# A fused attention and mixture-of-depths kernel: rows of four batches transposed by TensorE in place of DMA, their one-hot rows made by GpSimd, and a new hand-written order

## The chip, the cores and the metric

The kernel runs on one core of one Trainium2 chip. A core has five engines with an instruction stream each: TensorE (PE in the profile, with its weight loads as PEld), VectorE (DVE), ScalarE (ACT), GpSimd (POOL) and SyncE (SP). They work side by side and wait for each other by semaphores. Sixteen DMA engines move data for all of them; a DMA is issued by one of the instruction streams (here POOL for nearly all loads and stores, SP for the transposes). The metric is the device time of one execution in microseconds, lower is better.

## The reference

Eight batches of twelve heads, a sequence of 448 and a head size of 64. The attention takes the square of a Relu in place of a softmax:

```
scores = q k^T / 8
attn   = max(scores, 0)^2 / 448
x      = attn v            # heads side by side: [8, 448, 768]
```

On x, a mixture of depths follows. For each batch, 128 of the 448 tokens (those with the highest gate score `x . w_gate`) go through an MLP, and its result is added to their rows:

```
s   = x . w_gate                       # [8, 448]
idx = the 128 largest of s[b]
ye  = max(x[b, idx] w1, 0) w2          # 768 -> 1024 -> 768
out = x;  out[b, idx] += sigmoid(s[b, idx]) * ye
```

Inputs and output are fp32; the kernel works in bf16 with fp32 accumulation.

## The kernel before, in words

**Units.** The attention is cut into 24 units of four heads (u = 0 to 23), three to a batch. The sequence is cut into NC = 7 chunks of 64 keys. Each unit goes through these steps, named as in the order list:

- `Lq`, `Lk`, `Lv` (L95 to L105): GpSimd issues the loads, with a cast from fp32 to bf16. q, k and v tiles come from rings of seven buffers, so the load for unit u + 7 must wait until unit u's tile has been read by PE.
- `T` (L194): 28 groups of small PE transposes turn q and k into PSUM; `TE` copies them to SBUF (`qkt`, L131 or L135, in the helper `put`).
- `S` (L213): the score matmuls of one chunk, `R` (L131): Relu from PSUM to SBUF by ScalarE, 168 in all; `Q` (L228): the square by VectorE, for chunks 0 to 3 and 4 to 6 of a unit; `V` (L237): the matmul with v; `X` (L131 or L137): the result out of PSUM, scaled, as columns of x transposed (`xT_sb`, [feature, token]).
- `XB` (L258): two DMA transposes issued by SP bring the unit's 256 features from `xT_sb` into row form (`x_sb`, [token, feature]). Functions `XT` and `XE`, which would do this by TensorE and an eviction, exist in the code and are not in the order.

**Batches.** When the three units of a batch are through, the class `Moe` handles it: `g` (L297) gate scores by matmul, replicated over partitions; `bc` and `col`/`colE` (L306) bring them to SBUF as rows and as columns; `rk` (L316) gives each token's rank by comparing its score with all others; `hot` (L322) makes a one-hot row for each token by comparing its rank with 1 to 128; `sel` (L329) turns that into row numbers; `xe` (L341) gathers the chosen rows by a matmul of `x_sb` with the one-hot matrix, and `xeE` evicts them; `h` (L360), `hE`, `gt` (L372), `sig`, `y` (L382) and `yE` are the MLP with its gate. `ST` (L278) stores the rows of x, two DMAs a batch, and `ADD` (L392) adds the MLP's rows to the output in DRAM by an indirect, accumulating DMA.

`xe` needs the whole batch in `x_sb`, and so all six transposes of the batch, as well as the four `hot` rows.

**The order.** The schedule is manual. One list, `ORDER`, names every step of every engine in the order in which it is issued: each engine, and each queue, executes its own steps in the order of the list, and a step that waits holds up everything behind it on the same engine. The arguments say what is worked on and where: `S,4,3,6` is the scores of unit 4, chunk 3, into PSUM banks 6 and 7; `R,4,3` its Relu; a last letter A, D or P names ScalarE, VectorE or GpSimd. PSUM has eight banks, and the list says which step uses which. All data of one batch flows through a chain across engines (PE, ACT, DVE, DMA, PE), so the list interleaves several units and batches.

Of the kernel before, what the change touches and what calls it, by code (L numbers as in the profile page):

```python
# [19 lines left out]
def kernel(  # L20
# [178 lines left out]
    def TE(u, part=None, eng="D"):  # L199
        if u not in qkt:  # L200
            qkt[u] = qt_pool.tile([128, 2, 2, NC, P], BF16, name="qkt")
        for s in range(2) if part is not None else (slice(0, 2),):
            w = (slice(None), s) if part is None else (slice(None), s, part)
            r = "p s t c n -> p s (t c n)" if part is None else "p c n -> p (c n)"
            put(eng, qkt[u][w].rearrange(r), t_ps[u][w].rearrange(r))
# [11 lines left out]
    GROUPS = ((0, 1, 2, 3), (4, 5, 6))  # L217

    def R(u, c, eng="A"):
        g = [i for i, cs in enumerate(GROUPS) if c in cs][0]  # L220
        if (u, g) not in r_sb:
            r_sb[u, g] = r_pool.tile([128, len(GROUPS[g]), 2, S], BF16, name=f"r_sb{len(GROUPS[g])}")
        put(eng, r_sb[u, g][:, GROUPS[g].index(c)], s_ps.pop((u, c))[:, :, :S], func=AF.Relu)

    def Q(u, g):
        r = r_sb.pop((u, g))
        a = a_sb[u, g] = a_pool.tile([128, len(GROUPS[g]), 2, S], BF16, name=f"a_sb{len(GROUPS[g])}")
        nc.vector.tensor_tensor(out=a, in0=r, in1=r, op=ALU.mult)  # L228

    def V(u, g, at=None):  # L230
        if g == 0:
            o_ps[u] = banks(at, 2)
        for i, c in enumerate(GROUPS[g]):
            a = a_sb[u, g][:, i]
            for s, j, bank, col in ((0, 0, 0, 0), (1, 0, 0, 1), (1, 1, 1, 0), (0, 1, 1, 1)):
# [1 line left out]
                nc.tensor.matmul(out=o_ps[u][64 * col:64 * col + 64, bank, :S],  # L237
                                 lhsT=v_sb[u][rows, j, c, :], rhs=a[rows, j, :], start=(c == 0),
                                 stop=(c == NC - 1), skip_group_check=True)
# [169 lines left out]
    colE,0,D V,3,0,4 rk,0,3 R,4,3 S,4,4,1 V,3,1 rk,0,1 R,4,4 T,5,0,6 hot,0,3,D Lv,10,0 hot,0,1,D X,3,A rk,0,0
    S,4,2,2 S,4,5,0 R,4,2 rk,0,2 S,4,6,4 T,5,1 R,4,5 hot,0,0,D hot,0,2,D Lk,12 TE,5 xe,0,3,1,3 R,4,6  # L410
    xe,0,0,1,2 Lv,6,1 xe,0,4,1 xe,0,1,1 xe,0,5,1 Lv,7,0 xe,0,2,1 xeE,0,D,1 sel,0,7 xeE,0,A,0 S,5,3,5 Lq,9
    Q,4,1 S,5,0,0 gt,0,4 R,5,0 Lv,7,1 h,0,0,1,3 h,0,4,1,2 sig,0 Lq,10 h,0,1,1 R,5,3 Q,4,0 h,0,5,1 S,5,2,0
    S,5,1,5 h,0,6,1 R,5,1 h,0,2,1 selE,0,D h,0,7,1 R,5,2 h,0,3,1 V,4,0,4 hE,0,A,0 Q,5,0 hE,0,A,1 S,5,4,0
    S,5,5,6 V,4,1 R,5,4 T,6,0,2 X,4,A S,5,6,0 T,6,1 R,5,6 XB,4 g,1,0,1,5 TE,6 y,0,0,0,2,4 R,5,5 g,1,1,1
    y,0,0,2,2 Q,5,1 S,6,0,0 S,6,1,2 V,5,0,6 R,6,0 R,6,1 y,0,0,4,2 S,6,2,0 V,5,1 R,6,2 T,7,0,2 X,5,D Lv,12,0
    S,6,3,0 T,7,1 Lv,9,0 R,6,3 XB,5 g,1,2,1 TE,7 Lq,11 y,0,0,6,2 bc,1,A S,6,5,6 yE,0,A,0 Lk,10 XB,3 Q,6,0
    col,1 R,6,5 S,6,4,2 y,0,1,0,2,4 R,6,4 S,6,6,0 y,0,1,2,2 R,6,6 S,7,1,6 colE,1,D S,7,0,2 rk,1,0 y,0,1,4,2
    R,7,1 T,8,0,0 rk,1,3 R,7,0 S,7,2,6 rk,1,2 y,0,1,6,2 R,7,2 T,8,1 rk,1,1 S,7,4,2 yE,0,A,1 S,7,5,6 R,7,4 TE,8
    S,7,6,4 R,7,5 S,7,3,2 hot,1,2,D S,8,1,0 Q,6,1 R,7,3 V,6,0,6 R,7,6 S,8,3,2 Q,7,0 V,6,1 R,8,1 T,9,0,4
    Lv,13,1 X,6,A T,9,1 Lv,10,1 R,8,3 hot,1,0,D S,8,0,6 hot,1,3,D V,7,0,0 hot,1,1,D Lk,14 TE,9 R,8,0  # L420
    xe,1,3,1,3 Lv,8,0 xe,1,0,1,2 Q,7,1 S,8,6,4 Lk,16 S,8,2,6 R,8,6 xe,1,1,1 xe,1,4,1 Lq,13 xe,1,2,1 R,8,2
    xe,1,5,1 xeE,1,D,0 S,9,0,4 Lk,11 V,7,1 xeE,1,A,1 S,8,4,6 Lq,14 R,9,0 X,7,D h,1,4,1,2 h,1,0,1,3 Lv,12,1
    R,8,4 h,1,5,1 Q,8,0 XB,7 S,8,5,4 S,9,2,0 S,9,1,6 R,8,5 h,1,1,1 h,1,6,1 XB,6 R,9,2 h,1,2,1 h,1,7,1 Q,8,1
    R,9,1 T,10,0,4 h,1,3,1 hE,1,A,1 sel,1,0 hE,1,D,0 gt,1,7 T,10,1 selE,1,D sig,1 S,9,3,2 TE,10 Lk,17 S,9,6,0
    R,9,3 y,1,0,0,2,6 g,2,0,1,7 Lv,9,1 R,9,6 y,1,0,2,2 Q,9,0 Lv,11,1 S,10,0,4 V,8,0,2 R,10,0 S,9,4,0 V,8,1
    R,9,4 S,9,5,4 X,8,D Lv,15,1 y,1,0,4,2 R,9,5 S,10,1,0 ST,0,1 g,2,1,1 R,10,1 Q,9,1 XB,8 y,1,0,6,2 Lq,12
    S,10,3,2 S,10,2,4 R,10,3 T,11,0,0 Lv,15,0 yE,1,D,0 T,11,1 R,10,2 ST,1,0 S,10,4,2 TE,11 y,1,1,0,2,6 R,10,4
    Lv,11,0 g,2,2,1 y,1,1,2,2 Q,10,0 bc,2,A ST,0,0 S,10,6,4 S,11,1,0 R,10,6 y,1,1,4,2 Lk,18 col,2 y,1,1,6,2
    R,11,1 Lv,14,0 S,11,0,4 V,9,0,2 colE,2,D yE,1,A,1 Lk,13 rk,2,2 R,11,0 S,10,5,6 V,9,1 rk,2,1 R,10,5 Lv,16,0
    rk,2,0 T,12,0,0 X,9,A S,11,2,4 rk,2,3 T,12,1 R,11,2 S,11,3,2 hot,2,0,D V,10,0,6 hot,2,1,D R,11,3 hot,2,2,D  # L430
    hot,2,3,D TE,12 xe,2,0,1,5 xe,2,3,1,4 S,11,4,2 xe,2,1,1 Q,10,1 R,11,4 xe,2,4,1 xe,2,2,1 xe,2,5,1 xeE,2,A,0
    S,11,5,0 S,11,6,2 xeE,2,D,1 V,10,1 R,11,6 h,2,0,1,5 X,10,A Lv,17,1 sel,2,4 XB,9 h,2,4,1,3 R,11,5 selE,2,D
    Lv,13,0 h,2,1,1 Q,11,0 S,12,1,6 Lq,15 h,2,2,1 R,12,1 h,2,5,1 Lq,17 h,2,3,1 h,2,6,1 Q,11,1 hE,2,A,0 ST,2,0
# [99 lines left out]
```

## Time and profile before

| | |
|---|---|
| median of three runs | 256.56 us (255.26 to 257.10) |
| the profiled execution | 256.13 us |
| its span, first to last instruction | 254.4 us |
| mean granted TensorE clock | 0.881 of full speed |
| mean DMA rate | 162 GB/s, 41.11 MB |

How to read it: the span is cut by engine. Busy time is the time in which an engine executes instructions; what an engine waited for is listed beside the instruction that waited, with the tile that came last. A row such as `x_sb<-xT_sb` names the tile written and the tile read. The chain of waits is followed back from the last instruction; a piece on it isn't necessarily time in which nothing else happened, so it is compared with the timeline of the engine that waited. In tables by stretch, the last three columns are the granted TensorE clock (1.00 is full speed), the DMA load (packet time over the time of 16 engines; over 1 when packets of several queues overlap) and GB/s.

### The profile page before, as it was taken

The numbers are of one execution on the slowest core, as the hardware profiler recorded it, in microseconds if no ns is written. First come the engines' busy times: TensorE is split into PE (matmuls) and PEld (weight loads), VectorE is DVE, ScalarE is ACT, GpSimd is POOL, SyncE is SP. The second block draws the span as 40 slices with busy tenths as digits, with TensorE's granted clock in tenths as the row PEclk, the third lists the DMA queues.
The fourth block names the chain that finished last, engine by engine and source line by source line (L and its number), as shares of the span: only waits on it lengthen the run. The fifth ranks groups of instructions, "written<-read, shape, count | busy, mean of one in ns | idle before, by whom it ended". The sixth has DMA issues, their size and how long they took to land.

```text
span 254.4 us, 8167 instructions
## 1 busy us (share of the span) xinstructions
PE 190.4 (75%) x3614; PEld 118.4 (47%) x3614; DVE 163.2 (64%) x235; ACT 174.7 (69%) x236; POOL 97.2 (38%) x134
## 2 busy tenths in 40 slices
...
GB/s 169 196 200 153 174 188 183 171 197 202 93 161 132 171 5 199 291 155 66 159 272 100 103 136 166 164 285 261 149 203 121 124 250 81 151 202 83 232 63 52
DMA packets 53828, 41.11 MB, mean 162 GB/s; under 512 B 28960, under 2 KB 48416, under 8 KB 53792
## 3 DMA queue, kind: packets, MB, share of 16 engines
q0 software_dynamic: 26320, 33.37, 75.8%
q1 hardware_dynamic: 27184, 6.76, 25.9%
...
HBM read 39.32 MB, written 14.16 MB: 210 GB/s over the span
## 4 chain that ended last, share of the span: by engine, by line
PE 37%; DMA 25%; ACT 21%; issue 6%; SPq 4%; DVE 3%; POOLq 1%; DVEq 0%; ACTq 0%
DMA x_sb<-xT_sb 20%; ACT r_sb L131 16%; PE ps_all L213 8%; PE ps_all L237 8%; PE ps_all L360 7%; PE ps_all L341 5%; PE ps_all L382 5%; SPq L258 4%; DMA q_sb<-in_q_dram 2%; ACT xT_sb L131 2%; PE ps_all L297 2%; DMA out_dram<-gye,idx 2%; DVE xT_sb L137 1%; PE ps_all L194 1%; DVE qkt L135 1%
## 5 line engine op out<-in xcount | busy, mean ns | idle before, releaser
L131 ACT ACTIVATE r_sb<-ps_all 128x896 bf16<-128x896 f32 x168 | 143.6, 941 | 20.0 <-PE ps_all L213 18.8
L228 DVE TENSOR_TENSOR a_sb<-r_sb 128x2688 bf16<-128x2688 bf16 (+1 forms) x48 | 86.7, 1816 | 8.4 <-ACT r_sb L131 7.9
L213 PE MATMUL ps_all<-qkt 64*64 64x448 bf16 x672 | 64.2, 387 | 11.3 <-ACT r_sb L131 8.1
L105 POOL DMA_DIRECT2D v_sb<-in_v_dram x48 | 31.2, 662 | 75.3 <-PE ps_all L237 45.9
L237 PE MATMUL ps_all<-a_sb,v_sb 64*64 64x448 bf16 x672 | 44.1, 368 | 2.6 <-ACT r_sb L131 1.8
L213 PEld LDWEIGHTS <-qkt 64*64 64x64 bf16 x672 | 23.8, 109 | 37.1 <-issue 28.7
L341 PE MATMUL ps_all<-hot_sb,x_sb 128*128 128x128 bf16 x192 | 17.6, 249 | 30.7 <-DMA x_sb<-xT_sb 27.6
L135 DVE COPY qkt<-ps_all 128x1792 bf16<-128x1792 bf16 (+1 forms) x25 | 25.7, 1030 | 9.6 <-PE ps_all L194 8.4
L341 PEld LDWEIGHTS <-x_sb 128*128 128x128 bf16 x192 | 13.7, 112 | 35.7 <-DMA x_sb<-xT_sb 30.1
L131 ACT ACTIVATE xeT<-ps_all 128x384 bf16<-128x384 f32 x11 | 5.3, 503 | 35.6 <-PE ps_all L341 35.6
L237 PEld LDWEIGHTS <-v_sb 64*64 64x64 bf16 x672 | 22.1, 110 | 14.4 <-issue 7.6
L382 PE MATMUL ps_all<-w_sb,hT 128*128 128x384 bf16 x128 | 28.3, 328 | 0.5 <-DVE hT L133 0.3
L278 POOL DMA_DIRECT2D out_dram<-x_sb x16 | 11.0, 688 | 45.4 <-DMA x_sb<-xT_sb 34.8
L360 PE MATMUL ps_all<-xeT,w_sb 128*128 128x128 bf16 x384 | 28.2, 232 | 0.0
L360 PEld LDWEIGHTS <-w_sb 128*128 128x128 bf16 x384 | 24.2, 105 | 5.4 <-issue 4.9
L135 DVE CAST xeT<-ps_all 128x384 bf16<-128x384 f32 x5 | 2.8, 558 | 35.5 <-PE ps_all L341 35.5
L95 POOL DMA_DIRECT2D q_sb<-in_q_dram x23 | 18.8, 840 | 7.5 <-DVE hot_sb L322 2.7
...
L392 POOL DMA_INDIRECT out_dram<-gye,idx x8 | 14.3, 1784 | 14.1 <-ACT gye L131 11.3
L137 DVE TENSOR_SCALAR xT_sb<-ps_all 128x896 bf16<-128x896 f32 (+1 forms) x12 | 12.6, 1051 | 8.1 <-PE ps_all L237 5.9
L382 PEld LDWEIGHTS <-hT 128*128 128x128 bf16 x128 | 10.2, 97 | 11.8 <-issue 5.7
L297 PE MATMUL ps_all<-xT_sb,wg_rep 128*128 128x448 bf16 x48 | 13.0, 353 | 0.6 <-DVE xT_sb L137 0.2
(111 smaller groups left out, 157.2 us busy)
## 6 DMA issues: line engine op xcount, KB each, us to landing
out_dram<-x_sb POOLq DMA_DIRECT2D x8, 768.0 KB, 12.3
...
x_sb<-xT_sb SPq DMA_TRANSPOSE x48, 6.9
```

Of the source, the lines that this page charges most:

```text
L95: nc.gpsimd.dma_start(out=new(q_sb, u, "q_sb"), in_=heads(q, u).rearrange("(j s) (p c) d -> (s p) j (c d)", j=2, c=NC))
L99: nc.gpsimd.dma_start(out=new(k_sb, u, "k_sb"), in_=heads(k, u).rearrange("(j s) (p c) d -> (s p) j (c d)", j=2, c=NC))
L105: nc.gpsimd.dma_start(out=new(v_sb, u, "v_sb")[s * P:(s + 1) * P], in_=heads(v, u)[hs].rearrange("j (p c) d -> p j (c d)", c=NC))
L131: nc.scalar.activation(out=out_, in_=in_, func=func or AF.Copy, scale=scale)
L135: nc.vector.tensor_copy(out=out_, in_=in_)
L213: nc.tensor.matmul(out=ps[to:to + 64, j, :S], lhsT=qkt[u][rows, s, 1, c, :], rhs=qkt[u][rows, s, 0, :, :], start=True, stop=True, skip_gro ...
L228: nc.vector.tensor_tensor(out=a, in0=r, in1=r, op=ALU.mult)
L237: nc.tensor.matmul(out=o_ps[u][64 * col:64 * col + 64, bank, :S], lhsT=v_sb[u][rows, j, c, :], rhs=a[rows, j, :], start=(c == 0), stop=(c ...
L297: nc.tensor.matmul(out=self.sc[:, 0, :S], lhsT=wg_rep[:, m, :], rhs=self.xT[:, m, :S], start=(m == 0), stop=(m == NM - 1), skip_group_chec ...
L341: nc.tensor.matmul(out=self.ps["xe", m // 3][:, 0, m % 3 * 128:m % 3 * 128 + 128], lhsT=x_rows[self.b][:, i, m * 128:(m + 1) * 128], rhs=s ...
L360: nc.tensor.matmul(out=self.ps["h", f // 4][:, 0, f % 4 * 128:f % 4 * 128 + 128], lhsT=w1_sb[:, m, f * 128:(f + 1) * 128], rhs=self.xeT[:, ...
L382: nc.tensor.matmul(out=self.ps["y", n][:, 0, :384], lhsT=self.hT[:, i, :], rhs=w2_sb[:, i, n * 384:n * 384 + 384], start=(i == 0), stop=(i ...
```

## The change

1. **Order.** The whole `ORDER` list is written anew: positions, PSUM banks and in part the engines of the steps. The number of attention steps stays (168 `S` and `R`, 48 `Q`, `V` and `T`, 46 `Lq` and `Lk`, 48 `Lv`).
2. **Transposes.** For units 0 to 11 (batches 0 to 3) `XB` is replaced by `XT` and `XE`: eight TensorE transposes of 128x128 into one PSUM bank and one eviction of 128x1024 bf16 (ten by VectorE, two by ScalarE). Units 12 to 23 keep `XB`, so 24 of 48 DMA transposes stay.
3. **One-hot rows.** The 24 `hot` of batches 0 to 5 are made by GpSimd, in the same stream as its DMA issues; the eight of batches 6 and 7 stay with VectorE.
4. **Engines of small steps.** `X`: 15 on ScalarE, 10 on VectorE (13 and 12 before). `bc`: 5 and 3 (7 and 1). `colE`: 4 and 4 (0 and 8). `selE`: 5 and 3 (0 and 8). `hE`: 9 and 7 (10 and 6). `Cast`: 2 and 2 (3 and 1).
5. **Coarser pieces in the list.** `xe` comes in 16 steps of three 128-column blocks (48 before), `h` in 32 of two, `y` in 32 of four, `g` in 16; the matmuls in them are the same.
6. **Tiles.** `r_sb` and `a_sb` become one tile for each unit in place of one for each group of chunks. `bc_` becomes a constant tile padded to 512 columns, so that `col` and `colE` work on full 128 partitions (one `colE` copy in place of two). `TE` in parts copies q or k of both halves by one instruction.

The code of it, without the list:

```
+    bc_sb = [const.tile([128, NB * 128], FP32, name=f"bc_sb{i}") for i in range(2)]
...
+            for t in bc_sb:
+                nc.vector.memset(t[0:1, S:], 0.0)
...
+        r = "p s t c n -> p s (t c n)"
+        w = slice(0, 2) if part is None else slice(part, part + 1)
+        put(eng, qkt[u].rearrange(r)[:, w], t_ps[u].rearrange(r)[:, w])
...
+        if u not in r_sb:
+            r_sb[u] = r_pool.tile([128, NC, 2, S], BF16, name="r_sb")
+        put(eng, r_sb[u][:, c], s_ps.pop((u, c))[:, :, :S], func=AF.Relu)
...
+        if u not in a_sb:
+            a_sb[u] = a_pool.tile([128, NC, 2, S], BF16, name="a_sb")
+        cs = groups(u)[g]
+        cs = slice(cs[0], cs[-1] + 1)
+        nc.vector.tensor_tensor(out=a_sb[u][:, cs], in0=r_sb[u][:, cs], in1=r_sb[u][:, cs], op=ALU.mult)
...
-            put(eng, self.cols[:, :3], self.sc[:, 0, S:S + 3])
-            put(eng, self.cols[:64, 3:], self.sc[:64, 0, S + 3:S + 4])
+            put(eng, self.cols, self.sc[:, 0, S:S + NB])
```

The two functions that enter the order, unchanged in the code:

```
    def XT(u, at):
        b, w = divmod(u, NU)
        ps = x_ps[u] = banks(at, 1, BF16)
        for n in range(2):
            for i in range(NB):
                nc.tensor.matmul(out=ps[:, 0, (n * NB + i) * 128:(n * NB + i + 1) * 128],
                                 lhsT=xT_sb[b % NX][:, 2 * w + n, i * 128:(i + 1) * 128], rhs=ident,
                                 is_transpose=True, start=(n + i == 0), stop=(n + i == NB),
                                 skip_group_check=True)

    def XE(u, eng):
        b, w = divmod(u, NU)
        dst = rows_of(b)[:, :, w * 256:(w + 1) * 256].rearrange("p i (n d) -> p n i d", n=2)
        put(eng, dst, x_ps.pop(u)[:, 0, :].rearrange("p (n i d) -> p n i d", n=2, i=NB))
```

Two stretches of the list, around batches 0 and 4. Before:

```
... Q,1,1 Lq,6 R,2,2 V,1,0,0 XB,0 W1,2 R,2,3 ... XB,1 R,2,5 ... R,3,4 XB,2 S,3,5,1 ...
... hot,0,0,D hot,0,2,D Lk,12 TE,5 xe,0,3,1,3 R,4,6 xe,0,0,1,2 ...
... R,14,3 XB,12 T,15,0,4 ... Q,15,0 XB,14 ... R,15,6 XB,13 y,3,0,2,2 col,4 ...
... sel,4,7 ST,3,1 xe,4,0,1,6 R,17,4 ...
```

After:

```
... W1,1 XT,0,5 R,3,0 Lq,7 S,3,1,6 S,2,5,2 XE,0,D ... XT,2,6 bc,0,A S,3,6,2 XE,2,D ...
... XT,1,5 R,4,6 rk,0,2 hot,0,0,P S,5,5,2 R,5,5 XE,1,D S,4,4,0 hot,0,2,P ... Q,4,0 xe,0,0,3,6 ...
... R,14,1 xe,3,0,3,5 XB,12 Q,13,1 ... Lv,19,0 XB,13 V,14,0,2 ... hE,3,D,0 XB,14 S,15,6,2 ...
... S,18,0,6 X,15,D xe,4,3,3,2 Lq,21 ...
```

More of the change, by code (lines that the diff above doesn't have):

```diff
@@ L201, in TE @@
             qkt[u] = qt_pool.tile([128, 2, 2, NC, P], BF16, name="qkt")
[L202 to L205, printed above, removed]
+        r = "p s t c n -> p s (t c n)"
+        w = slice(0, 2) if part is None else slice(part, part + 1)
+        put(eng, qkt[u].rearrange(r)[:, w], t_ps[u].rearrange(r)[:, w])
     def SC(u, c, at):
@@ L215, in SC, with groups @@
                                  skip_group_check=True)
-    GROUPS = ((0, 1, 2, 3), (4, 5, 6))
+    GROUPS = [[0, 1, 2, 3], [4, 5, 6]]
+    LAST = [[0, 1, 2, 3], [4, 5, 6]]
+    def groups(u):
+        return LAST if u == B * NU - 1 else GROUPS
     def R(u, c, eng="A"):
[L220 to L223, printed above, removed]
+        if u not in r_sb:
+            r_sb[u] = r_pool.tile([128, NC, 2, S], BF16, name="r_sb")
+        put(eng, r_sb[u][:, c], s_ps.pop((u, c))[:, :, :S], func=AF.Relu)
     def Q(u, g):
-        r = r_sb.pop((u, g))
-        a = a_sb[u, g] = a_pool.tile([128, len(GROUPS[g]), 2, S], BF16, name=f"a_sb{len(GROUPS[g])}")
-        nc.vector.tensor_tensor(out=a, in0=r, in1=r, op=ALU.mult)
+        if u not in a_sb:
[3 more added lines that the diff above has]
+        nc.vector.tensor_tensor(out=a_sb[u][:, cs], in0=r_sb[u][:, cs], in1=r_sb[u][:, cs], op=ALU.mult)
     def V(u, g, at=None):
@@ L409 @@
[L409 to L433, printed above, removed]
@@ new lines @@
+    R,6,2 T,7,1 V,5,0,0 Lv,8,0 TE,7 R,6,3 S,6,1,2 V,5,1 Lk,12 R,6,1 S,6,0,6 X,5,D Lv,9,0 R,6,0 S,6,4,2
+    g,1,0,2,4 Lk,10 R,6,4 Q,6,0 Lq,10 S,6,6,0 S,7,1,6 R,6,6 XT,3,2 Lq,12 g,1,2,1 R,7,1 S,7,0,0 bc,1,D XT,4,3
+    R,7,0 XE,3,D S,6,5,5 col,1 R,6,5 XE,4,D S,7,2,0 XT,5,2 R,7,2 colE,1,D rk,1,3 gt,0,7 y,0,0,0,4,3 sig,0
+    XE,5,A rk,1,0 hot,1,3,P T,8,0,6 S,7,3,4 S,7,5,0 rk,1,1 T,8,1 R,7,3 y,0,1,0,4,2 TE,8 hot,1,1,P R,7,5
+    S,7,4,4 y,0,0,4,4 Lv,11,1 R,7,4 Q,6,1 S,8,1,0 hot,1,0,P S,8,0,6 yE,0,A,0 y,0,1,4,4 R,8,1 ST,0,0 sel,0,3
@@ new lines @@
+    g,2,2,1 ST,0,1 h,1,6,2 R,10,4 bc,2,D Lv,10,0 XT,7,4 R,10,0 hE,1,D,1 Lq,14 col,2 S,9,5,1 XE,7,D colE,2,A
+    gt,1,3 Lv,11,0 R,9,5 sel,1,0 T,11,0,6 rk,2,1 S,10,3,4 Lq,13 T,11,1 sig,1 R,10,3 S,10,5,1 TE,11 y,1,0,0,4,3
+    ST,1,0 R,10,5 S,10,2,4 Lv,12,0 Q,9,1 y,1,0,4,4 R,10,2 Lv,12,1 S,10,1,6 T,12,0,1 R,10,1 V,9,0,4 hot,2,1,P
+    rk,2,3 yE,1,A,0 T,12,1 S,11,0,6 rk,2,0 selE,1,A hot,2,3,P V,9,1 R,11,0 Lk,14 rk,2,2 XT,8,3 X,9,A
+    y,1,1,0,4,0 hot,2,0,P XE,8,D S,10,6,6 hot,2,2,P TE,12 S,11,1,4 R,10,6 y,1,1,4,4 Lq,16 xe,2,0,3,3 R,11,1
@@ new lines @@
+    rk,3,1 S,13,1,4 S,13,4,2 R,13,3 y,2,1,0,4,7 rk,3,0 hot,3,1,P R,13,1 y,2,0,0,4,0 Lq,18 rk,3,2 R,13,4
+    y,2,1,4,4 Lv,13,0 Q,12,1 T,14,0,5 yE,2,A,1 Lv,18,1 S,13,5,3 S,13,6,1 T,14,1 R,13,5 sel,2,7 Lk,17 TE,14
+    y,2,0,4,4 selE,2,A R,13,6 Lv,15,0 XT,10,4 rk,3,3 S,13,2,6 yE,2,A,0 hot,3,2,P T,15,0,2 R,13,2 S,14,2,0
+    XE,10,D Lv,14,0 T,15,1 R,14,2 TE,15 S,14,3,4 hot,3,0,P V,12,0,6 R,14,3 hot,3,3,P S,14,5,0 Q,13,0 V,12,1
+    Lq,17 R,14,5 S,14,1,3 xe,3,3,3,2 ST,2,1 X,12,A S,14,0,0 Lv,16,1 xeE,3,D,1 R,14,1 xe,3,0,3,5 XB,12 Q,13,1
```

128 lines of the change are left out of this document (65 added, 63 removed).

## The prediction

> **What bounds the kernel now.** First the busy times of the profile's page:
>
> ```profile
> PE 190.4 (75%) x3614; PEld 118.4 (47%) x3614; DVE 163.2 (64%) x235; ACT 174.7 (69%) x236; POOL 97.2 (38%) x134
> ...
> q0 software_dynamic: 26320, 33.37, 75.8%
> q1 hardware_dynamic: 27184, 6.76, 25.9%
> ...
> x_sb<-xT_sb SPq DMA_TRANSPOSE x48, 6.9
> ```
>
> No engine is full over the span of 254.4 us. TensorE (PE) is the fullest: 64.0 us of the span are its idle time. The two large DMA queues together hold packets for 101.7% of the span of 16 engines, so the DMA engines are loaded nearly throughout; a quarter of that load is q1, the 48 transposes of XB. Next, what the idle time was spent on, by the waits of PE and the longest lines of the POOL queue:
>
> ```profile
> PE ps_all L341 <- DMA x_sb<-xT_sb: 27.6, 6, 10.6
> PE ps_all L213 <- ACT r_sb L131: 8.1, 24, 0.8
> ...
> POOL v_sb L105 <- PE ps_all L237: 45.9, 7, 11.5
> ```
>
> The largest single wait of PE is the gather matmul (`xe`, L341), which needs the rows of a batch back from the DMA transpose. ScalarE's Relu is the second, in 24 small pieces. The third line shows what such a stall does to the loads: GpSimd stands before a load whose ring slot PE hasn't read yet. The chain of waits, in order of time, says where:
>
> ```profile
> 42.43 13.71 DMA x_sb<-xT_sb
> ...
> 76.50 13.53 DMA x_sb<-xT_sb
> ...
> 157.35 17.09 DMA x_sb<-xT_sb
> ...
> 193.31 7.71 DMA x_sb<-xT_sb
> ...
> 238.98 5.60 DMA out_dram<-gye,idx
> ```
>
> Four transposes take 52.0 us of the chain: those of batches 0, 1, 4 and 5. The chain may run through a transfer while PE does other work, so the price is read from PE's own timeline:
>
> ```profile
> 50.46 1.03 PE L341 MATMUL ps_all<-hot_sb,x_sb 128*128 128x128 bf16 x8 [8.64 <-DMA x_sb<-xT_sb]
> 53.09 1.03 PE L341 MATMUL ps_all<-hot_sb,x_sb 128*128 128x128 bf16 x8 [1.59 <-DMA x_sb<-xT_sb]
> 56.19 1.03 PE L341 MATMUL ps_all<-hot_sb,x_sb 128*128 128x128 bf16 x8 [2.06 <-DMA x_sb<-xT_sb]
> ...
> 85.83 0.40 PE L341 MATMUL ps_all<-hot_sb,x_sb 128*128 128x128 bf16 x4 [1.36 <-DMA x_sb<-xT_sb]
> ...
> 90.08 1.89 PE L341 MATMUL ps_all<-hot_sb,x_sb 128*128 128x128 bf16 x16 [3.34 <-DMA x_sb<-xT_sb]
> ...
> 117.18 0.79 PE L341 MATMUL ps_all<-hot_sb,x_sb 128*128 128x128 bf16 x11 [2.15 <-issue]
> ...
> 174.49 2.31 PE L341 MATMUL ps_all<-hot_sb,x_sb 128*128 128x128 bf16 x20 [10.56 <-DMA x_sb<-xT_sb]
> ...
> 235.98 1.50 PE L341 MATMUL ps_all<-hot_sb,x_sb 128*128 128x128 bf16 x24
> ```
>
> PE lost 12.3 us in batch 0 (8.64 + 1.59 + 2.06), 4.7 in batch 1 (1.36 + 3.34), 2.15 in batch 2 (a pause inside the gather; the view names no releaser), 10.56 in batch 4. Batch 5's 7.71 us of the chain cost it nothing of note: there is no such row. Then the table by stretches, for what follows a stall:
>
> ```profile
> 50.00:60.00 10.00, 5.88 (x62) 4.64 (x63) 3.10 (x3) 2.07 (x4) 5.85 (x9) 0.50 1.26 197
> ...
> 90.00:100.00 10.00, 9.92 (x177) 7.14 (x178) 6.74 (x7) 5.86 (x9) 5.14 (x8) 0.77 0.59 93
> ...
> 170.00:180.00 10.00, 5.51 (x53) 3.84 (x54) 2.84 (x3) 2.22 (x3) 3.03 (x3) 0.50 1.11 251
> ...
> 233.00:254.40 21.40, 10.93 (x145) 8.52 (x141) 4.33 (x14) 4.31 (x10) 4.52 (x4) 0.86 0.52 113
> ```
>
> The columns are PE, PEld, DVE, ACT and POOL busy, the granted clock, the DMA load and GB/s. After each long wait PE works at a granted clock of 0.50, so the wait costs twice: the idle time, and slow matmuls behind it.
>
> **The change part by part.**
>
> *Transposes of batches 0 to 3 leave the DMA* (XB of units 0 to 11: 24 of 48 DMA_TRANSPOSE). The waits of batches 0, 1 and 2 lose their cause: 12.3 + 4.7 + 2.15 = 19.1 us. The slow clock behind them goes too: (1 - 0.50) x 5.88 = 2.9 us in the first row, (1 - 0.77) x 9.92 = 2.3 in the second, 5.2 together. Bounds: the whole 24.3, or nothing where another wait takes the place.
>
> *TensorE transposes in their place* (XT: 12 units x 8 = 96 matmuls of 128x128). The last row of the timeline has 24 gather matmuls of that size in 1.50 us, 62 ns each at full clock: 96 x 0.0625 = 6.0 us on the fullest engine, which I charge in full. If nothing of them overlapped, the mean duration of one gather matmul, 249 ns below, would give 23.9; the 672 small transposes of k, issued in the same way, fill 11.7 us in all (17 ns each, at a duration of 199), so transposes do overlap and I stay with 6.0.
>
> ```profile
> L135 DVE COPY qkt<-ps_all 128x1792 bf16<-128x1792 bf16 x23 | 25.0, 1086 | 5.7 <-PE ps_all L194 4.6 <-ACT xT_sb L131 0.5 <-ACT r_sb L131 0.3
> ...
> L341 PE MATMUL ps_all<-hot_sb,x_sb 128*128 128x128 bf16 x192 | 17.6, 249 | 30.7 <-DMA x_sb<-xT_sb 27.6 <-issue 2.2 <-ACT r_sb L131 0.9
> ...
> L194 PE MATMUL ps_all<-ident,k_sb 64*64 64x64 bf16 x672 | 11.7, 199 | 2.3 <-issue 1.4 <-ACT qkt L131 0.9
> L131 ACT ACTIVATE xT_sb<-ps_all 128x896 bf16<-128x896 f32 x12 | 11.4, 946 | 0.0
> ...
> L162 POOL TENSOR_SCALAR_AFFINE_SELECT tie<-tie 128x1792 bf16<-128x1792 bf16 x1 | 2.9, 2858 | 0.1
> ...
> L322 DVE TENSOR_SCALAR hot_sb<-slot_row,rank__1176 128x128 bf16<-128x128 bf16 x3 | 0.7, 245 | 0.0
> ...
> L135 DVE COPY qkt<-ps_all 128x448 bf16<-128x448 bf16 x2 | 0.7, 386 | 3.9 <-PE ps_all L194 3.9
> ...
> L131 ACT ACTIVATE xT_sb<-ps_all 128x448 bf16<-128x448 f32 x1 | 0.5, 544 | 0.6 <-PE ps_all L237 0.6
> ...
> L150 POOL TENSOR_SCALAR_AFFINE_SELECT ident<-ident 128x128 bf16<-128x128 bf16 x1 | 0.3, 317 | 0.1
> ```
>
> *Their evictions* (XE: 10 on VectorE, 2 on ScalarE, 128x1024 bf16). VectorE: 386 ns for 448 and 1086 for 1792 elements give 0.521 ns an element, so 0.69 us, 6.9 in all. ScalarE: 544 for 448 and 946 for 896 give 0.897, so 1.06 us, 2.1 in all.
>
> *One-hot rows of batches 0 to 5 on GpSimd* (24 of 32 `hot`). VectorE loses 24 x 0.245 = 5.9 us, which pays for nearly all of its XE. On GpSimd the operation doesn't occur; the same shape in another operation took 0.317 us, 14 times its width 2.86, which bound it (7.6 to 69 us in all). I take 0.32: the shape is equal. GpSimd is idle for 157 of 254 us, so it lies beside other work. Without that cover a late hot delays `xe`, and each load behind it in the queue; that is the second last rival.
>
> *Small moves*: two X (0.946 each), half of the colE and five selE go to ScalarE, two bc leave it. With XE, ScalarE gains about 4 us. It is busy for 69% of the span, beside PE; the 4 us count only where ScalarE, not PE, sets the pace. I take 1 (0 to 4). The 24 issues that SP loses cost nothing, since SP has no other work there. Three of W2's four loads move back, to 14 to 16 Relus ahead of their first use, against 21 to 23 before: no charge, with the feed below as the bound.
>
> *The order*. Batches 4 to 7 keep their DMA transposes. Counted in the two orders, batch 4's last XB stands 11 Relu evictions ahead of its first gather before, 13 after; batch 5's 10 and 12, batch 6's 9 and 14. In time that is 13 x 0.94 = 12 us of ScalarE against landings of 6.9 us at the median and 17.09 at worst. Before, XB,13 and XB,14 were both in that last stretch; now XB,13 is 16 Relus ahead and XB,14 alone is last. Of batch 4's 10.56 us and its slow clock ((1 - 0.50) x 5.51 = 2.8), 13.3 in all, I take 11 as recovered; ends: 0 and 13.3. The rest of the new order can win at most the 8.1 us of Relu waits and lose as much, and I put 0.
>
> *Does the DMA feed a shorter run?* Packet time: 101.7% of 254.4 = 258.7 us; without half of q1 (32.9) it is 225.8. The last 21.4 us hold 0.52 x 21.4 = 11.1 of it, so the load ahead of the tail was (258.7 - 11.1) / 233.0 = 1.06. At the same load the changed kernel needs (225.8 - 11.1) / 1.06 + 21.4 = 223.9 us: just under the sum below, so no charge, but little room. [...]
>
> **Sum**: 254.4 - 19.1 - 5.2 - 11.0 + 6.0 + 1.0 = 226.1 us of span. The profiled run took 256.13 us, 1.7 more than its span, so 227.8; the median of the runs before, 256.56, is 0.4 above the profiled one. I say 228.
>
> **The rivals.** *The DMA binds the second half*: 24 transposes still go among loads and stores. For it: over 233 us the trace kept up 1.06 and no more, and batch 4 shows a landing of 17 us. If the load can be held at 1.0 only, the feed ends at 214.7 + 21.4 = 236.1, with 1.7 outside 238; if batch 4's stall returns whole, 228 + 11 = 239. Against: two to five more Relus of lead. I call it 239.
>
> *All of it goes*: batch 4's last 2.3 and the Relu waits of 8.1 vanish: 228 - 10.4 = 217.6. Against: ScalarE gets more work.
>
> *The transposes don't pipeline*: 23.9 us in place of 6.0 gives 246. Against: the 672 transposes of k in 11.7 us. [...]
>
> *GpSimd's queue locks up (slower)*: a hot waits for VectorE's rank in the queue that issues every load, so loads behind it are late, PE waits for them, and the next rank is later still. The POOL wait above averages 45.9 / 7 = 6.6 us; once in each of six batches is 39 us on 228 - 5 for a part that overlaps, 262. It decides where a load reaches its use with less lead than that wait. Against: from unit 3 on, the new order has each load at least 8 Relus (7.5 us) ahead of its use, where the order before had 7.
>
> *It doesn't do what it says*: the waits reappear as waits for XE, hot or loads, and the sum is nought: 256.
>
> **How the numbers follow.** Forecast 0.50; DMA binds 0.24; all goes 0.14; no pipelining 0.04; locked queue 0.04; nought 0.04. About 1% is what a measurement can tell (the runs before spread from 255.26 to 257.1). Faster: 0.50 + 0.24 + 0.14 + 0.04 = 0.92; same 0.04; slower 0.04. The range takes in 217 and 239 with the ScalarE bound of 4 on top: 216 to 243.
>
> **What would show it.** Right: no wait of L341 on x_sb in batches 0 to 3; XT's 96 matmuls near 6 us; granted clock near 1 from 30 us until the tail; 24 transposes and q1 near 13% of the old span. Wrong: PE waits for XE or hot of several us per batch; loads that land after their T or V; a batch 4 or 5 gather that still waits ten us; a mean XT spacing near 250 ns.

## The result and the profile after

The changed kernel takes 228.68 us (median of 4 runs, 227.77 to 232.18), the kernel before 256.61 us beside it (4 runs, 255.26 to 257.10): a ratio of 0.892, with an interval of 0.886 to 0.899. The forecast was 228.0, with a range of 216 to 243.

Some executions are disturbed and a few per cent longer, among them the first profiled one of the changed kernel (232.18 us) and those of the first two experiments below, so the rows after the change are from a second profile of the same kernel, with a span of 226.0 us, unless the first is named. The forecast of the span was 226.1. That the two agree to 0.1 is in part luck: several terms were off, in both directions, as the points below show.

Busy times, queues and transposes of the page after:

```profile
PE 185.7 (82%) x3710; PEld 119.2 (53%) x3710; DVE 162.9 (72%) x207; ACT 177.5 (79%) x244; POOL 122.8 (54%) x158
...
q0 software_dynamic: 26320, 33.37, 82.5%
q1 hardware_dynamic: 14128, 3.61, 15.8%
q8 instruction: 29, 0.48, 0.8%
...
x_sb<-xT_sb SPq DMA_TRANSPOSE x24, 7.8
```

TensorE has 96 more matmuls and yet is busy for 4.7 us less. Its idle time falls from 64.0 us (254.4 - 190.4) to 40.3 (226.0 - 185.7). Both together are the 28.4 us of the span: 23.7 of idle time, 4.7 of busy time. The matmuls added take 7.4 us (below), so the others became 12.1 us shorter, while the mean granted clock went from 0.881 to 0.973. That 0.973 flatters. It counts the stretch from 10 to 20 us as 1.00, and the score matmuls there take 569 ns each:

```profile
L215 PE MATMUL ps_all<-qkt 64*64 64x448 bf16 x48 | 6.0, 569 | 2.3 <-ACT r_sb L132 1.5 <-DVE qkt L136 0.8
```

They take the same 569 ns in the first profile, which has 0.50 for that stretch, 568 in the kernel before, and 362 ns in the first profile from 70 to 80 us, where its clock is 1.00. So the start runs as slowly as before, and what the clock gained lies behind it.

The waits of PE after:

```profile
PE ps_all L215 <- ACT r_sb L132: 6.2, 18, 0.7
PE ps_all L347 <- DMA x_sb<-xT_sb: 5.2, 3, 2.3
PE ps_all L197 <- issue: 4.3, 3, 2.0
...
PE ps_all L347 <- POOL hot_sb L328: 2.2, 2, 1.1
```

The gather (L341 before, L347 now) waits 5.2 us for transposed rows in place of 27.6: 22.4 of the 23.7 us. PE's timeline has what is left, in batches 4, 6 and 7:

```profile
145.27 1.62 PE L347 MATMUL ps_all<-hot_sb,x_sb 128*128 128x128 bf16 x16 [2.26 <-DMA x_sb<-xT_sb]
...
194.25 1.51 PE L347 MATMUL ps_all<-hot_sb,x_sb 128*128 128x128 bf16 x20 [1.69 <-DMA x_sb<-xT_sb]
...
207.17 0.40 PE L347 MATMUL ps_all<-hot_sb,x_sb 128*128 128x128 bf16 x4 [1.25 <-DMA x_sb<-xT_sb]
```

In the chain of waits, the long pieces of transposes and stores near the end are these:

```profile
184.92 9.73 DMA x_sb<-xT_sb
...
201.19 5.93 DMA x_sb<-xT_sb
...
209.80 6.50 DMA out_dram<-x_sb
```

Batches 0 to 3, whose rows TensorE transposes, have no such wait. The granted clock (third column from the right) and PE's busy time (second number) in the table by stretches:

```profile
50.00:60.00 10.00, 7.80 (x166) 5.17 (x163) 6.85 (x6) 7.72 (x10) 4.68 (x8) 1.00 1.22 197
90.00:100.00 10.00, 10.00 (x162) 7.12 (x157) 8.92 (x9) 8.68 (x13) 4.78 (x8) 1.00 0.86 154
...
170.00:180.00 10.00, 9.53 (x212) 6.57 (x204) 8.66 (x8) 9.78 (x15) 8.66 (x10) 1.00 0.92 146
```

The same three stretches of the kernel before had clocks of 0.50, 0.77 and 0.50. The work in them isn't the same, since the changed kernel is ahead; before, waits of 12.3, 4.7 and 10.56 us for rows led into them or lay in them, and now there is none. Around batch 4's wait of 2.26 us the clock still falls:

```profile
140.00:150.00 10.00, 6.63 (x84) 4.25 (x83) 4.82 (x4) 6.08 (x9) 9.51 (x12) 0.83 1.30 189
```

What is new is in GpSimd's waits, of which the largest is this one:

```profile
POOL hot_sb L328 <- DVE trash L322: 44.0, 10, 13.3
```

GpSimd stands before a one-hot row until VectorE has made the rank.

### The profile page after: what moved, and what is told of

The parts are those of the page before. It is cut to its first block, busy times and chain, and to the rows that moved or that the text cites. A ratio compares the mean times of both kernels' runs of the same rounds, so it can differ in the third digit from the quotient of the medians.

```text
span 230.5 us, 8305 instructions
## 1 busy us (share of the span) xinstructions
PE 188.2 (82%) x3710; PEld 119.6 (52%) x3710; DVE 162.9 (71%) x207; ACT 177.3 (77%) x244; POOL 121.6 (53%) x158
## 4 chain that ended last, share of the span: by engine, by line
PE 40%; ACT 18%; DMA 13%; DVE 10%; issue 9%; POOL 4%; POOLq 1%; SPq 0%; ACTq 0%; DVEq 0%
ACT r_sb L132 16%; PE ps_all L244 10%; PE ps_all L215 9%; DMA x_sb<-xT_sb 8%; PE ps_all L366 6%; DVE a_sb L235 5%; PE ps_all L388 4%; PE ps_all L197 3%; DMA q_sb<-in_q_dram 3%; DMA out_dram<-x_sb 3%; PE ps_all L347 3%; PE ps_all L305 3%; DVE qkt L136 2%; POOL hot_sb L328 2%; PE ps_all L273 1%
## 5 line engine op out<-in xcount | busy, mean ns | idle before, releaser
L366 PE MATMUL ps_all<-xeT,w_sb 128*128 128x128 bf16 x384 | 25.3, 219 | 0.8 <-ACT xeT L132 0.4
L366 PEld LDWEIGHTS <-w_sb 128*128 128x128 bf16 x384 | 22.1, 98 | 5.1 <-issue 4.2
L388 PE MATMUL ps_all<-w_sb,hT 128*128 128x384 bf16 x128 | 24.6, 327 | 0.1
L322 DVE SCALAR_TENSOR_TENSOR trash<-bc_sb,cols,tie 128x448 bf16<-128x448 f32 (+1 forms) x32 | 21.9, 684 | 3.1 <-ACT cols L132 2.2
L285 POOL DMA_DIRECT2D out_dram<-x_sb x16 | 14.3, 896 | 9.4 <-DMA x_sb<-xT_sb 8.0
L347 PE MATMUL ps_all<-hot_sb,x_sb 128*128 128x128 bf16 x192 | 13.4, 219 | 5.1 <-DMA x_sb<-xT_sb 3.1
L132 ACT ACTIVATE xT_sb<-ps_all 128x896 bf16<-128x896 f32 (+1 forms) x15 | 13.8, 918 | 2.9 <-PE ps_all L244 2.8
L138 DVE TENSOR_SCALAR xT_sb<-ps_all 128x896 bf16<-128x896 f32 (+1 forms) x10 | 10.4, 1042 | 7.7 <-PE ps_all L244 5.8
L347 PEld LDWEIGHTS <-x_sb 128*128 128x128 bf16 x192 | 11.0, 98 | 7.6 <-DMA x_sb<-xT_sb 3.7
L197 PE MATMUL ps_all<-ident,q_sb 64*64 64x64 bf16 x672 | 10.7, 198 | 4.6 <-issue 2.5
```

What stands on the lines that cost most here:

```text
L132: nc.scalar.activation(out=out_, in_=in_, func=func or AF.Copy, scale=scale)
L322: nc.vector.scalar_tensor_tensor(out=trash[:n], in0=self.bc_[:n, :S], scalar=self.cols[:n, i:i + 1], in1=tie[:n, i, :], op0=ALU.subtract, ...
L347: nc.tensor.matmul(out=self.ps["xe", m // 3][:, 0, m % 3 * 128:m % 3 * 128 + 128], lhsT=x_rows[self.b][:, i, m * 128:(m + 1) * 128], rhs=s ...
L366: nc.tensor.matmul(out=self.ps["h", f // 4][:, 0, f % 4 * 128:f % 4 * 128 + 128], lhsT=w1_sb[:, m, f * 128:(f + 1) * 128], rhs=self.xeT[:, ...
L388: nc.tensor.matmul(out=self.ps["y", n][:, 0, :384], lhsT=self.hT[:, i, :], rhs=w2_sb[:, i, n * 384:n * 384 + 384], start=(i == 0), stop=(i ...
```

## The experiments

The theory at the outset: the gain is the transposes' waits and the clock behind them, on the new order's lead for batch 4; the one-hot rows on GpSimd cost nothing. The main rivals: the order alone brings the gain; the DMA engines bind; GpSimd's held queue costs time. All medians are of runs interleaved with the kernel before on one chip. Ratios are to that kernel, whose own runs spread from 249 to 264 us, so only the medians of kernels that were measured together can settle a question of 1 or 2%. There were three such groups: the two kernels with exchanged transposes, the first with one-hot rows by VectorE and the first with all transposes by TensorE; then the change again, one-hot rows by both, all transposes by TensorE with one-hot rows by VectorE, and the kernel without stores; last, one-hot rows by VectorE again, the tail and the 14 warm-up matmuls. The 228.68 us of the change itself belong to none of them.

| kernel | median us | runs, spread | ratio to before |
|---|---|---|---|
| XB back in batches 0 to 3 | 246.38 | 4, 243.88 to 248.32 | 0.961 [0.952, 0.971] |
| old order with XT | 248.03 | 4, 245.28 to 251.71 | 0.967 [0.958, 0.977] |
| one-hot rows by VectorE | 225.15 | 6, 222.83 to 228.95 | 0.878 [0.870, 0.886] |
| the same, measured again | 226.11 | 6, 224.32 to 229.74 | 0.892 [0.885, 0.899] |
| one-hot rows by both | 222.62 | 6, 220.20 to 225.88 | 0.882 [0.863, 0.902] |
| the change again | 228.84 | 6, 227.80 to 234.34 | 0.911 [0.895, 0.928] |
| all transposes by TensorE | 226.41 | 6, 225.40 to 227.67 | 0.886 [0.881, 0.892] |
| that, one-hot rows by VectorE | 227.38 | 6, 226.42 to 230.24 | 0.908 [0.892, 0.923] |
| without the stores of x | 216.47 | 4, 216.00 to 222.06 | 0.863 [0.835, 0.891] |
| tail transposes by TensorE | 227.03 | 6, 224.16 to 229.33 | 0.899 [0.890, 0.907] |
| 14 warm-up matmuls | 229.22 | 1 | |

**The transposes alone, taken out of the change.** The new order with DMA transposes in all batches:

```
- XT,0,5 R,3,0 Lq,7 S,3,1,6 S,2,5,2 XE,0,D
+ XB,0 R,3,0 Lq,7 S,3,1,6 S,2,5,2
  (so for units 0 to 11)
```

> The changed kernel with DMA transposes for all 24 units: XT becomes XB at its place, XE is dropped. Waits (mine): the gathers of batches 0 to 2 wait for x_sb again and the slow clock follows, 17 + 5 us against 7.4 us of PE work saved, so 238 to 246 us, with L347 waiting on x_sb in at least two of batches 0 to 3. Order alone: the new order has enough lead for the DMA, so 221 to 228 us and no such waits.

It took 246.38 us: 17.7 more than the changed kernel (0.961 against 0.892 as ratios). The forecast's terms for this part come to 18.3 net (19.1 + 5.2 - 6.0). The wait is back on PE in batch 0:

```profile
46.23 0.49 PE L347 MATMUL ps_all<-hot_sb,x_sb 128*128 128x128 bf16 x6 [2.64 <-POOL hot_sb L328]
...
53.79 0.61 PE L347 MATMUL ps_all<-hot_sb,x_sb 128*128 128x128 bf16 x4 [7.06 <-DMA x_sb<-xT_sb]
...
57.42 1.46 PE L347 MATMUL ps_all<-hot_sb,x_sb 128*128 128x128 bf16 x12 [2.13 <-DMA x_sb<-xT_sb]
```

But it isn't back as it was. Batch 1 has no such wait, batch 2 one of 0.43 us, and the gather's waits for rows come to 8.0 us more than in the change (5.2), not to 17.0 more:

```profile
PE ps_all L347 <- DMA x_sb<-xT_sb: 13.2, 5, 7.1
```

About as much again is in PE's pauses without a releaser (12.0 us in all, 4.3 in the change). The rest of this profile's 20.6 us of longer span is in waits for Relu (9.0 us, 6.2 in the change) and for one-hot rows (3.5 and 2.2), and in a slower clock. So the agreement of 17.7 with 18.3 is in part luck.

Batch 4, whose rows come by DMA in both orders, has next to none left:

```profile
164.68 1.07 PE L347 MATMUL ps_all<-hot_sb,x_sb 128*128 128x128 bf16 x16 [0.32 <-DMA x_sb<-xT_sb]
```

So the new order takes batch 4's wait from 10.56 to 0.32 us, with all 48 DMA transposes in place. It is worth 10.8 us (257.17 to 246.38, measured together), about what the forecast gave it: 11.0 for batch 4's lead less 1.0 for ScalarE. "The new order" here is all of the change but the transposes: the one-hot rows on GpSimd, the small moves, the coarser steps and the tiles are in this kernel too, and weren't taken apart.

**The transposes alone, put into the old order.**

```
- XB,0 W1,2 R,2,3 ... W2,2 R,2,4
+ XT,0,3 W1,2 R,2,3 ... W2,2 XE,0,D R,2,4
  (so for units 0 to 11; one-hot rows stay with VectorE)
```

> The kernel before, in its own order, with TensorE transposes for units 0 to 11 at the place of XB, evicted by VectorE some five items later. Waits (mine): the gather waits of batches 0 and 1 go and nothing else, so about 256 - 17 - 5 + 7 = 241 us (237 to 245), with batch 4's wait still there. Order alone: 250 to 257 us, because the order causes the waits.

It took 248.03, 9.1 less than the kernel before beside it (257.17), and missed what I expected. The gather's waits in batches 0 and 1 are gone, as wanted; batch 4's is not:

```profile
162.69 2.31 PE L341 MATMUL ps_all<-hot_sb,x_sb 128*128 128x128 bf16 x20 [11.67 <-DMA x_sb<-xT_sb]
```

and PE now also waits for ScalarE to clear the bank that a transposition wants:

```profile
PE ps_all L341 <- DMA x_sb<-xT_sb: 14.8, 3, 11.7
...
PE ps_all L266 <- ACT r_sb L131: 4.0, 5, 1.0
```

So relief of the DMA queues by half of the transposes doesn't shorten batch 4's wait (11.67 us here, 10.56 before), while the new order without that relief does (0.32): the wait belongs to the order. How the order does it is seen in the chain of waits, by batch 4's last transpose (its issue, and how long until it landed), in this kernel, in the new order with DMA transposes, and in the change:

```profile
144.33 18.31 DMA x_sb<-xT_sb
...
153.83 10.81 DMA x_sb<-xT_sb
...
131.18 14.05 DMA x_sb<-xT_sb
```

PE is ready for these rows where its wait begins: 6.7, 10.5 and 11.8 us behind the issue, against 6.6 in the kernel before, whose landing took 17.09. What the landing takes beyond that is the wait. So the lead grew by 3.9 to 5.2 us, and the landing became shorter by 6.3 to 3.0. Lead alone doesn't bring it. Why the landing is shorter no run shows; the forecast noted that XB,13 and XB,14 no longer stand together in the last stretch.

The two parts alone bring 9.1 and 10.8 us, together 28: about 8 us are worth something only jointly. One piece of that is shown, the 4.0 us that `XT` waits for banks where the order has no place for it; the rest I can't assign.

**Where the one-hot rows are made.** First all 24 back to VectorE:

```
- hot,0,1,P
+ hot,0,1,D
  (so for all 24 of batches 0 to 5)
```

> The changed kernel with all 32 one-hot rows on VectorE again. Three theories. Cover (mine): GpSimd's one-hot rows lie beside other work and VectorE is not what sets the pace, so 227 to 231 us, no change beyond 1%. Held queue: the rows cost time on GpSimd, because PE waited 1.9 us for them and loads stood behind them for up to 13.5 us, so 223 to 226 us. Relief: VectorE's 5.9 us count in full, so 232 to 235 us.

225.15 us, and 226.11 when it was measured again beside other kernels. That is 2.6 to 3.5 less than the change's 228.68, but never measured beside it, and as ratios to the kernel before the two are 0.878 and 0.892 against 0.892. It suggests that this part of the change costs time; the next kernel, measured beside the change, decides. Two causes were possible: GpSimd's work itself, or its wait at the head of the queue that issues the loads. The next kernel has the first without the second: VectorE makes the real rows, and GpSimd does the same operation in the same places on constants, so that it has nothing to wait for.

```
+ fixed = const.tile([128, 1], FP32)
+ spare = const.tile([128, CAP], BF16)
...
+ nc.vector.tensor_scalar(... as in hot ...)
+ if eng == "P":
+     nc.gpsimd.tensor_scalar(out=spare[:n], in0=slot_row[:n], scalar1=fixed[:n],
+                             scalar2=None, op0=ALU.is_equal)
```

> The changed kernel in which VectorE makes all one-hot rows, and GpSimd makes a row of the same size at each of the 24 places too, from a constant into a spare tile, so that it waits for no rank. Held queue: it is the wait for VectorE's ranks in front of the loads that cost, so the time is as without GpSimd's rows, 223 to 227 us, and the idle DMA stretch near 100 us is gone. Own time: it is GpSimd's 24 us of work in the queue and its contention with VectorE, so 228 to 231 us.

> The changed kernel as it is, beside the others on the same chip: 227 to 230 us by every theory. It gives the base for the other three.

222.62 against 228.84 for the unaltered change measured together with it; the two spreads don't touch. GpSimd was busier (124.1 us against 122.8) and the kernel faster by 6.2, so it isn't the work. How the wait acts, in GpSimd's timeline of the changed kernel:

```profile
94.09 0.74 POOL L100 DMA_DIRECT2D k_sb<-in_k_dram  x1
108.09 0.99 POOL L328 TENSOR_SCALAR hot_sb<-slot_row,rank__2435 128x128 bf16<-128x128 bf16 x1 [13.27 <-DVE trash L322]
109.05 0.76 POOL L96 DMA_DIRECT2D q_sb<-in_q_dram  x1
```

For 13.27 us no load is issued. The table by stretches (last two columns: DMA load, GB/s) shows the DMA engines run dry and then crowded:

```profile
100.00:110.00 10.00, 9.25 (x166) 5.39 (x162) 9.74 (x15) 9.68 (x14) 1.90 (x3) 1.00 0.01 2
...
120.00:130.00 10.00, 7.83 (x229) 5.16 (x222) 6.68 (x7) 7.45 (x12) 6.64 (x9) 1.00 1.50 241
```

and with one-hot rows by both, the same stretch is filled:

```profile
100.00:110.00 10.00, 9.25 (x170) 5.32 (x172) 9.77 (x16) 9.68 (x14) 6.87 (x8) 1.00 1.05 215
```

PE is as busy in that stretch in both (9.25 of 10 us), so the loss comes later. The crowded DMA reaches batch 4: here is the median of its six transposes from issue to landing, in the change (116 to 132 us) and with one-hot rows by both (116 to 129 us):

```profile
x_sb<-xT_sb SPq DMA_TRANSPOSE x6, 13.0
...
x_sb<-xT_sb SPq DMA_TRANSPOSE x6, 6.5
```

Batch 4's gather, which waits 1.02 us for its one-hot row and 2.26 for x in the changed kernel, has neither wait with one-hot rows by both:

```profile
138.29 1.51 PE L353 MATMUL ps_all<-hot_sb,x_sb 128*128 128x128 bf16 x24
```

Nor has any other batch's gather: the 5.2 us of waits for rows and the 2.2 us for one-hot rows (batches 3 and 4) are all gone there. So the wait for the rank acts in two ways, late loads and late one-hot rows, and no run tells their prices apart. The kernel with one-hot rows by VectorE does wait in batch 4 (2.47 us for x), so that place isn't the whole of it.

**The other transposes too.** All 24 units by TensorE, no DMA transpose left; then the same with the one-hot rows by VectorE:

```
- XB,12
+ XT,12,bank ... XE,12,D
  (so for units 12 to 23; in the second kernel also hot,b,i,P to hot,b,i,D)
```

> The changed kernel with TensorE transposes for units 12 to 23 too, so no DMA transpose at all. Waits (mine): 3.1 us of waits on x_sb go and 7.4 us of PE work come, part of it in the tail where PE has room, so 226 to 232 us. DMA load: the remaining transposes slow the loads, the stores and PE's own instruction stream, so taking them away wins 5 us or more, 218 to 224 us, and the unexplained pauses of PE (2.5 and 3.45 us) shrink.

> TensorE transposes for all 24 units and all one-hot rows on VectorE. Additive: the two gains seen alone (about 3.5 and 2.3 us) add up, 222 to 224 us. VectorE full: 8.2 us of evictions and 5.9 us of one-hot rows more than in the changed kernel make VectorE the bound, 225 to 229 us.

226.41 and 227.38. The first lies 2.3 us under the change's 228.68, but it wasn't measured beside it, and the intervals of the two ratios overlap: what the 24 transposes that the change keeps cost it isn't clear of the noise. Its pauses of PE come to 3.5 us, 4.3 in the change. The second is 1.5 us under the change measured together with it (228.84), so the two gains, if they are gains, don't add up. The busiest engines of the second kernel:

```profile
PE 189.4 (84%) x3806; PEld 123.5 (55%) x3806; DVE 173.2 (77%) x243; ACT 177.0 (79%) x244; POOL 96.8 (43%) x134
```

VectorE has the evictions and the one-hot rows now, 10 us more than in the change. That speaks for the second of the two things that I expected, a full VectorE. That VectorE is the cause was not tested by itself.

**The stores, and the end.** One kernel has none of the 16 stores of x; another, from the one with one-hot rows by VectorE, has the last batch's transposes by TensorE.

```
- ST,0,0 ... ST,7,1          (the first)

- XB,21 ... XB,22 ... XB,23          (the second)
+ XT,21,1 XE,21,D ... XT,22,4 XE,22,D ... XT,23,7 XE,23,D
```

> The changed kernel without the 16 stores of x rows (ST), so the output holds the additions alone; 10.75 MB less for the DMA. Instruction stream: PE's pauses stand at every 128th matmul (index 92 to 94) because its next block of instructions comes late through loaded DMA engines; with less load they shrink from 8.1 us to under 3, and the time falls to 219 to 224 us. Fixed: the pauses are a cost of the block change itself, they stay at 6 us or more and the time is 226 us or more.

> The kernel with all one-hot rows on VectorE once more, as base for the next one: 222 to 227 us by every theory.

> All one-hot rows on VectorE, and TensorE transposes for batch 7 too (units 21 to 23), so that only batches 4 to 6 use the DMA. Tail: in the tail nothing hides a DMA transpose, and PE and VectorE have room there, so the gathers of batch 7 and its stores start 3 to 5 us earlier, 219 to 222 us. Covered: the end is set by the MLP and the additions, which start no earlier, so no change, 223 to 226 us.

Without stores 216.47 us, 12.4 less than the change beside it and more than I expected. A small part is the end itself. In the change the rows for the last `ADD` are ready at 214.4 us and it starts at 217.1, after a store that is a piece of 6.50 us on the chain; without stores they are ready at 205.8 and it starts at 206.1. That is 2.5 us. PE's last matmul ends 8.6 us sooner (213.8 and 205.2 us). Ahead of it the gather's waits for rows are gone (5.2 us in the change), those for one-hot rows fell from 2.2 to 0.8 and the pauses from 4.3 to 3.1, while the waits for Relu rose from 6.2 to 8.6.

With the last batch's transposes by TensorE 227.03 against 226.11: no gain. The chain's end with TensorE:

```profile
205.04 1.05 POOL out_dram L398
206.09 6.03 DMA out_dram<-x_sb
```

and with DMA:

```profile
204.98 1.05 POOL out_dram L398
206.03 6.57 DMA out_dram<-x_sb
```

The last store lands 0.5 us earlier with TensorE, but PE ends 1.0 us later (211.5 against 210.5 us), and the last `ADD` starts at 212.9 against 213.4. The kernel with DMA had no wait for rows in batch 7 to begin with, so this pair doesn't show what the 1.25 us of that wait in the change cost.

**What pauses PE with no releaser.** Batch 2's pause of 2.15 us, which I had put down to the transposes, was "<-issue". Such pauses stand in the change as well. In PE's timeline, a group of 28 transposes of q is cut in two:

```profile
51.82 0.35 PE L197 MATMUL ps_all<-ident,q_sb 64*64 64x64 bf16 x22
54.12 0.25 PE L197 MATMUL ps_all<-ident,q_sb 64*64 64x64 bf16 x6 [1.94 <-issue]
```

Counted in matmuls from the start, PE had executed 862 before this one, 2397 before another (2.03 us), and 1629 before batch 2's in the kernel before. These are 94, 93 and 93 over a multiple of 128. If the pause belongs to the count and not to the step, 16 warm-up matmuls less (step `N`, at the start) must move it 16 matmuls down the program, to after 6 transposes of q, 4 matmuls of scores and 6 transposes of k:

```
- N,1,30
+ N,1,14
```

> The changed kernel with 14 in place of 30 warm-up matmuls, so that each later matmul has an index 16 lower. Instruction stream: the pauses without a releaser stay at index 92 to 94 of each 128, that is 16 matmuls later in the program than before, not inside the same group of unit 7's transposes. Program: they stay at the same place of the program, so the index becomes 76 to 78. The time is 226 to 231 us by both.

The timeline of that kernel:

```profile
53.06 0.23 PE L197 MATMUL ps_all<-ident,k_sb 64*64 64x64 bf16 x6
54.59 0.38 PE L197 MATMUL ps_all<-ident,k_sb 64*64 64x64 bf16 x22 [1.29 <-issue]
```

and, from its start to the pause, the table by stretches for PE alone (busy time, matmuls in brackets, granted clock, DMA load, GB/s):

```profile
0.00:54.57 54.57, 39.56 (x862) 1.00 1.02 166
```

It did: the pause is now after 6 of the 28 transposes of k, and the count ahead of it is again 862. The pause goes with the count of instructions, not with the program's step. The kernel with `XB` back in batches 0 to 3, which has 24 matmuls less ahead of this place, says the same: its first pause (1.78 us) is again behind 862 matmuls. Most counts of that kind bring no pause: the change has three, in 3710 matmuls.

## Why the prediction was right, and where it wasn't

**Batches 0 and 1 (17.0 of the 19.1 us, and 5.2 of clock).** Right for the change: the waits are gone and the clock is 1.00 in both stretches. Putting the DMA transposes back into the new order costs 17.7 us where the terms gave 18.3, but that agreement is luck in part: only batch 0's wait returns in size (9.2 us for rows; 0.43 in batch 2), and pauses of PE make up much of the rest. So the new order alone would have removed batch 1's wait too.

**Batch 2 (2.15 us of the 19.1).** Wrong. The step that failed is "The waits of batches 0, 1 and 2 lose their cause", for batch 2. It has no releaser in the view because it isn't a wait for rows: PE pauses there behind 1629 matmuls, one of the counts above. The change has such pauses of 4.3 us in all (8.1 in its first profile), the kernel before of 3.6. The DMA queue listed as "instruction" (q8) moves 28 packets with 3614 matmuls (the kernel before), 29 with 3710 (the change), and 30 and 29 with 3806 (all transposes by TensorE; the same with one-hot rows by VectorE): about one packet for 128 matmuls, of about 16.5 KB (0.48 MB in 29). That agrees with the period of the pauses, but no run shows that PE waits for such a packet. Whether a loaded DMA makes them longer is open. In the new order they sum to 12.0 us with all 48 DMA transposes, 4.3 or 8.1 with 24, 3.5 with none and 3.1 without the stores, which suggests it; in the old order they sum to 3.6 with 48 and 1.4 with 24. But the two profiles of one kernel differ by 3.8.

**Batch 4 (11.0 of 13.3).** Right in that the order does it, and in size to about 1 us: 2.26 us of the wait are left, and (1 - 0.83) x 6.63 = 1.1 of slow clock, so that 9.9 of 13.3 came back. That it is the order, not the lighter DMA load, is shown by the two crossed kernels: 0.32 us with the new order alone, 11.67 with the transposes alone. The lead that the forecast gave it, 12 us, came as 11.8; but that is 5.2 more than before, and the other 3.0 of the 8.3 us that the wait lost are a landing of 14.05 in place of 17.09 us.

**TensorE's transposes (6.0 us).** The mechanism was right, the term low by 1.4. After, grouped by line and form:

```profile
L273 PE MATMUL ps_all<-ident,xT_sb 128*128 128x128 bf16 x96 | 7.4, 220 | 0.0
L136 DVE COPY x_sb<-ps_all 128x1024 bf16<-128x1024 bf16 x10 | 6.8, 685 | 0.9 <-PE ps_all L273 0.7
...
L132 ACT ACTIVATE x_sb<-ps_all 128x1024 bf16<-128x1024 bf16 x2 | 2.1, 1059 | 0.0
```

96 in 7.4 us are 77 ns each, at a duration of 220 ns, so they do overlap. They come in twelve groups of eight, 0.62 us a group, and eight gather matmuls in a row take 0.61 us in this trace too; the 62 ns of the forecast were from a row of 24. The rival without overlap (23.9 us) is refuted. The evictions came as worked out: 685 and 1059 ns against 0.69 and 1.06 us.

**One-hot rows on GpSimd (no cost).** Wrong twice. One was priced at 0.32 us, 7.6 in all, with a bound of 69; GpSimd's busy time rose by 25.6 us (97.2 to 122.8), about 1.1 each. Measured, two batches:

```profile
L328 POOL TENSOR_SCALAR hot_sb<-slot_row,rank__2435 128x128 bf16<-128x128 bf16 x3 | 2.2, 747 | 13.3 <-DVE trash L322 13.3
...
L328 POOL TENSOR_SCALAR hot_sb<-slot_row,rank__3556 128x128 bf16<-128x128 bf16 x3 | 4.8, 1601 | 13.6 <-DVE trash L322 13.6
```

In the kernel with one-hot rows by both, where GpSimd's copies wait for nothing, the view of that tile gives the least, middle and longest duration:

```profile
L334 POOL TENSOR_SCALAR spare<-slot_row,fixed x24: 593/643/2629, 28.5 to 142.0; 128x128 bf16<-128x128 bf16 x18, 64x128 bf16<-64x128 bf16 x6
```

In the first profile, all five one-hot rows over 1.2 us stand beside VectorE's square, which reads two operands; one of them, in GpSimd's timeline:

```profile
142.93 2.48 POOL L328 TENSOR_SCALAR hot_sb<-slot_row,rank__3054 128x128 bf16<-128x128 bf16 x1
```

and VectorE's timeline at that moment:

```profile
142.99 2.02 DVE L235 TENSOR_TENSOR a_sb<-r_sb 128x3584 bf16<-128x3584 bf16 x1
```

The other 19 of the first profile took 1.09 us at most. Why a comparison is longer beside the square, no run shows. But the extra time itself is hidden, as forecast: the kernel whose GpSimd does the same work without waiting is the fastest. What cost 3 to 6 us (6.2 where measured together) is the step "it lies beside other work": the wait for the rank stands in the queue that issues the loads, and late one-hot rows hold PE besides (2.2 us). That is the mechanism of the locked-queue rival, at a small part of its price (39 us there): PE is as busy as without the wait while no load is issued, so the loads have enough lead that it isn't held at once.

**ScalarE (1.0 us) and the rest of the order (0).** ScalarE's busy time rose by 2.8 us (4 forecast); the Relu waits of PE fell from 8.1 to 6.2. New are the 2.9 us of waits for rows in batches 6 and 7 (1.69 and 1.25), which the sum didn't have. These terms can't be told apart in the total.

**The DMA rival (239).** It showed in part only. Batch 4's gather waits 2.26 us in a stretch with a DMA load of 1.30, where the rival had its 11 us return whole. The packet time of q0 and q1 is 98.3% of 226.0 = 222.2 us, near the 225.8 forecast, so the engines are about as loaded as before, and the 12.4 us that the run without stores gains, 2.5 of them at the end, say that room is still paid for.

**The sum.** Charged too little were the held queue (3 to 6 us), the pause of batch 2 (2.15, which stays in another place), XT (1.4) and batch 4 (1.1). Credited too little was the clock: the matmuls that were there before got 12.1 us shorter, where the terms had 5.2, and at most 2.8 of batch 4's. Taken as in the forecast, (1 - clock) x busy time over all stretches of 10 us from 30 us on, the slow clock cost about 11 us before and 1 to 2 after, so an estimated 10 of the 12.1 are the clock; the rest isn't assigned. The Relu waits gave 1.9 more. That these come out even within 0.1 us is chance; they overlap, and I can't book the rest item by item.
